# A SwiGLU feed-forward kernel: its first eight accumulation groups ordered by contraction step, with loads cut to match

## The chip, the core and the metric

The kernel runs on one core of a Trainium2 chip. The metric is device time in microseconds (us) of one execution; the number to be predicted is the median of the runs of the changed kernel. TensorE (PE) multiplies matrices into PSUM, ScalarE (ACT) evaluates SiLU, VectorE (DVE) multiplies and copies, and SyncE (SP) issues DMAs.

## The reference

```python
B, S, D, F = 1, 2048, 512, 1376          # x: S x D; w_gate, w_up: D x F; w_down: F x D; all bfloat16
def reference(x, w_gate, w_up, w_down):
    g = silu(x @ w_gate)
    u = x @ w_up
    return (g * u) @ w_down
```

## The kernel before

Everything fits on the chip, and each input is loaded once. The tokens are cut into four chunks of 512 (index `c`), the hidden size F into ten full tiles of 128 columns (index `ft`) and a rest of 96, the contraction over D into four steps of 128 (index `dk`; the changed kernel's text calls it k).

**Up-projection.** For each chunk `c` and tile `ft`, PE makes two accumulation groups of four matmuls each: the gate group G (line 179) and the up group U (line 191). One matmul takes a 128x128 block of `w_sb` as its weights and streams 512 columns of `xT_sb`, the transposed x, into one PSUM bank. ACT turns a G bank into SiLU in `sg_sb` (line 261); DVE multiplies that by the U bank and writes `hT_sb` (line 284). G groups use banks 0 to 2 in turn, U groups banks 3 and 4. The order is four matmuls of G, then four of U, tile by tile. The rest of 96 columns is packed with part of w_up in one more group X per chunk (line 204), and two groups Y at the end (lines 215 and 220).

**Down-projection.** For each of the 16 token tiles of 128, PE accumulates eleven matmuls over F into bank 6 or 7 in turn (line 245), DVE copies the bank to `o_sb` (line 308), and SP stores it (line 156). The last token tile is done in two halves of 256 columns; ACT copies the first half (line 275).

**The start.** PE first runs `N_WARM = 11` matmuls on constants (line 167), which need no data. ACT loads its SiLU table and evaluates it once on a dummy (line 254). SP alone issues all loads, in this order: the transposing load of the first chunk of x, whole, 512 x 512 (line 128); then w_gate and w_up alternately in slabs of 1, 1, 2, 3 and 4 tiles, each slab with all four contraction steps (lines 116 and 123); 32 columns of w_up (line 140); the other three chunks of x; w_down in two DMAs (lines 145 and 146). Each load has a semaphore of its own, and PE waits for x's chunk and for a slab before its first matmul with it. So PE's first real matmul needs the whole first chunk of x (512 KB) and the first slab of w_gate (128 KB); the engines work through their programs in the written order, and nothing reorders the groups.

Of the kernel before, what the change touches and what calls it, by code (L numbers as in the profile page):

```python
# [9 lines left out]
N_WARM = 11  # L10


def bass_standalone__swiglu_ffn__prompt_kernel(nc, x, w_gate, w_up, w_down, out):
# [4 lines left out]
    NFT = (F + P - 1) // P  # L18
    NFF = F // P
    F_LAST = F - NFF * P  # L20
# [5 lines left out]
    assert D == 512 and S % SC == 0 and KD == 4 and TPC == 4 and F_LAST == 96 and NSC % 2 == 0  # L26
# [4 lines left out]
    UPT = F  # L31
# [4 lines left out]

    slabs = [(0, 1), (1, 2), (2, 4), (4, 7), (7, NFT)]
    slab_of = {}
    for si, (a, b) in enumerate(slabs):
        for ft in range(a, b):  # L40
            slab_of[ft] = si

    with ExitStack() as es:
# [9 lines left out]
        NSG = 3  # L53
# [3 lines left out]
        NOS = 3  # L57
        o_sb = [sb(f"o_sb{i}", [P, D], BF16) for i in range(NOS)]

        banks = [ps(f"bank{i}", [P, 512], FP32) for i in range(8)]  # L60
        NG = 3
        psG = [banks[0], banks[1], banks[2]]
        NU = 2
        psU = [banks[3], banks[4]]
        psX = banks[5]
        NO = 2
        psO = [banks[6], banks[7]]
        psY = [banks[0], banks[1]]

        s_xT = [sem(f"s_xT{c}") for c in range(NSC)]  # L70
        s_wg = [sem(f"s_wg{i}") for i in range(len(slabs))]
        s_wu = [sem(f"s_wu{i}") for i in range(len(slabs))]
        s_wut = sem("s_wut")
        s_wd = sem("s_wd")
        s_G = sem("s_G")
        s_U = sem("s_U")
        s_Gf = sem("s_Gf")
        s_Uf = sem("s_Uf")
        s_X = sem("s_X")
        s_Xa = sem("s_Xa")  # L80
        s_Xd = sem("s_Xd")
        s_Y = sem("s_Y")
        s_Yd = sem("s_Yd")
        s_O = sem("s_O")
        s_Of = sem("s_Of")
        s_Ofa = sem("s_Ofa")
        s_out = [sem(f"s_out{i}") for i in range(NOS)]

# [4 lines left out]
        o_groups = []  # L93
        for t in range(NST):
            if t == NST - 1:
                o_groups.append((t, 0, HD))
                o_groups.append((t, HD, HD))
            else:
                o_groups.append((t, 0, D))
        NOG = len(o_groups)  # L100

        NGU = NSC * NFF
        gu_list = [(c, ft) for c in range(NSC) for ft in range(NFF)]

        def og_buf(gi):
            return o_groups[gi][0] % NOS

        def yblk(c):
            return (0, 64) if c % 2 == 0 else (64, 128)

        block = es.enter_context(nc.Block(no_gpsimd_drain=True))

        def wg_slab_dma(eng, si):
            a, b = slabs[si]
            f0, f1 = a * P, min(b * P, F)
            return eng.dma_start(
                w_sb[:, :, f0:f1], w_gate[:, f0:f1].rearrange("(k p) f -> p k f", p=P)
            ).then_inc(s_wg[si], 16)

        def wu_slab_dma(eng, si):  # L120
            a, b = slabs[si]
            f0, f1 = a * P, min(b * P, F - 32)
            return eng.dma_start(
                w_sb[:, :, UPH + f0:UPH + f1], w_up[:, f0:f1].rearrange("(k p) f -> p k f", p=P)
            ).then_inc(s_wu[si], 16)

        def xT_dma(eng, c):
            return eng.dma_start_transpose(
                xT_sb[:, :, c * SC:(c + 1) * SC], xf[c * SC:(c + 1) * SC, :]
            ).then_inc(s_xT[c], 16)  # L130

        WD_TOTAL = 32

        @block.sync
        def _(sp):
            xT_dma(sp, 0)
            for si in range(len(slabs)):
                wg_slab_dma(sp, si)
                wu_slab_dma(sp, si)
            sp.dma_start(  # L140
                w_sb[:, :, UPT:UPT + 32], w_up[:, F - 32:F].rearrange("(k p) f -> p k f", p=P)
            ).then_inc(s_wut, 16)
            for c in range(1, NSC):
                xT_dma(sp, c)
            sp.dma_start(wd_sb[:, 0:NFF, :], w_down[0:NFF * P, :].rearrange("(k p) d -> p k d", p=P)).then_inc(s_wd, 16)
            sp.dma_start(wd_sb[0:F_LAST, NFF, :], w_down[NFF * P:F, :]).then_inc(s_wd, 16)
            n_store = [0] * NOS
            for gi, (t, c0, ncol) in enumerate(o_groups):
                ob = og_buf(gi)
                if gi == NOG - 2:  # L150
                    sp.wait_ge(s_Ofa, 1)
                elif gi == NOG - 1:
                    sp.wait_ge(s_Of, gi)
                else:
                    sp.wait_ge(s_Of, gi + 1)
                sp.dma_start(of[t * P:(t + 1) * P, c0:c0 + ncol], o_sb[ob][:, c0:c0 + ncol]).then_inc(s_out[ob], 16)
                n_store[ob] += 1
            for i in range(NOS):
                sp.wait_ge(s_out[i], 16 * n_store[i])

        @block.tensor
        def _(pe):
            seen_g = set()
            seen_u = set()
            seen_x = set()
            for i in range(N_WARM):
                pe.matmul(banks[7][:, :], lhsT=ones_w, rhs=ones_m, start=True, stop=True)  # L167
            n = 0
            for c in range(NSC):
                pe.wait_ge(s_xT[c], 16)  # L170
                for ft in range(NFF):
                    si = slab_of[ft]
                    if si not in seen_g:
                        pe.wait_ge(s_wg[si], 16)
                        seen_g.add(si)
                    if n >= NG:
                        pe.wait_ge(s_Gf, n - NG + 1)
                    for dk in range(KD):
                        ins = pe.matmul(  # L179
                            psG[n % NG][:, :], lhsT=w_sb[:, dk, ft * P:(ft + 1) * P],  # L180
                            rhs=xT_sb[:, dk, c * SC:(c + 1) * SC],
                            start=(dk == 0), stop=(dk == KD - 1),
                        )
                    ins.then_inc(s_G, 1)
                    if si not in seen_u:
                        pe.wait_ge(s_wu[si], 16)
                        seen_u.add(si)
                    if n >= NU:
                        pe.wait_ge(s_Uf, n - NU + 1)
                    for dk in range(KD):  # L190
                        ins = pe.matmul(  # L191
                            psU[n % NU][:, :], lhsT=w_sb[:, dk, UPH + ft * P:UPH + (ft + 1) * P],
                            rhs=xT_sb[:, dk, c * SC:(c + 1) * SC],
                            start=(dk == 0), stop=(dk == KD - 1),
                        )
                    ins.then_inc(s_U, 1)
                    n += 1
                if c == 0:
                    pe.wait_ge(s_wg[slab_of[NFT - 1]], 16)
                    pe.wait_ge(s_wut, 16)  # L200
                else:
                    pe.wait_ge(s_Xd, c)
                for dk in range(KD):
                    ins = pe.matmul(  # L204
                        psX[:, :], lhsT=w_sb[:, dk, XC0:XC0 + P],
                        rhs=xT_sb[:, dk, c * SC:(c + 1) * SC],
                        start=(dk == 0), stop=(dk == KD - 1),
                    )
                ins.then_inc(s_X, 1)
            pe.wait_ge(s_wu[slab_of[NFT - 1]], 16)  # L210
            pe.wait_ge(s_Gf, NGU)
            for pi in range(NSC // 2):
                a, b = 2 * pi, 2 * pi + 1
                for dk in range(KD):
                    pe.matmul(  # L215
                        psY[pi][0:64, :], lhsT=w_sb[:, dk, YC0:YC0 + 64],
                        rhs=xT_sb[:, dk, a * SC:(a + 1) * SC],
                        start=(dk == 0), stop=(dk == KD - 1), tile_position=(0, 0), skip_group_check=True,
                    )
                    ins = pe.matmul(  # L220
                        psY[pi][64:128, :], lhsT=w_sb[:, dk, YC0:YC0 + 64],
                        rhs=xT_sb[:, dk, b * SC:(b + 1) * SC],
                        start=(dk == 0), stop=(dk == KD - 1), tile_position=(0, 64), skip_group_check=True,
                    )
                ins.then_inc(s_Y, 1)
            pe.wait_ge(s_wd, WD_TOTAL)
            seen_c = set()
            for gi, (t, c0, ncol) in enumerate(o_groups):
                bb = gi % NO
                c = t // TPC  # L230
                if c not in seen_c:
                    pe.wait_ge(s_Uf, NFF * (c + 1))
# [104 lines left out]
```

## Time and profile before

| | |
|---|---|
| three timed runs | 122.66, 122.89 and 123.19 us; median 122.89 us |
| the profiled execution: first to last instruction (span) | 121.1 us |
| its own time from outside | not given; the median run lies 1.74 us above the span |
| PE busy | 117.9 us, 97% of the span, 550 matmuls |
| DVE, ACT busy | 43.8 us (36%), 30.2 us (25%) |
| DMA | 8.42 MB on one queue, nearly all loads in the first fifth of the span |
| granted TensorE clock | 1.000 |

The profile is one execution on the chip. "PEld" rows are the weight loads that precede matmuls; "SPq" rows are DMA issues on SP's queue. A DMA's "us to landing" runs from its issue to the arrival of its last byte's signal. Matmuls are pipelined: a row's duration is longer than the pitch at which matmuls follow each other, and the pitch is what adds up to time.

### The profile page before, as it was taken

To read this page: it belongs to the slowest core of one execution; us is meant where nothing else is said; L and a number is where in the kernel's file an instruction comes from. 1 tells how busy PE (TensorE), PEld (TensorE's weight loads), DVE (VectorE), ACT (ScalarE), POOL (GpSimd) and SP (SyncE) were. 2 spreads that over 40 slices of the span, in tenths; PEclk is the share of its full clock that TensorE was granted. 3 is DMA by queue.
4 is the path that set the end of the run, shared out by engine and by line. 5 is a ranking of instruction groups with operands and counts; after the bars stand their busy time and mean duration, and the time that the engine had idled before them with its cause. 6 is when DMAs were issued, how large, how long until landed. Compare 5 with 4: busy or idle time off the path is not lost.

```text
span 121.1 us, 1391 instructions
## 1 busy us (share of the span) xinstructions
PE 117.9 (97%) x550; PEld 53.3 (44%) x550; DVE 43.8 (36%) x64; ACT 30.2 (25%) x51; POOL 0.2 (0%) x4
## 2 busy tenths in 40 slices
PE   7999999999999999999999999999999999999991
PEld 2244444444444444444444444444444444444470
DVE  0024334444334444334444334467242233224221
ACT  4032333262333272333262333230000000000010
POOL 0000000000000000000000000000000000000000
PEclk9999999999999999999999999999999999999999
DMA  3999999900000000000000000000211211121121
GB/s 67 255 283 372 262 241 225 369 20 0 0 0 0 0 0 5 0 0 3 3 0 0 0 0 0 5 0 0 87 43 43 87 43 49 49 81 43 43 74 56
DMA packets 17990, 8.51 MB, mean 70 GB/s; under 512 B 11360, under 2 KB 17984, under 8 KB 17984
## 3 DMA queue, kind: packets, MB, share of 16 engines
q1 hardware_dynamic: 17984, 8.42, 25.6%
q8 instruction: 4, 0.07, 0.2%
q14 instruction: 2, 0.02, 0.0%
HBM read 4.23 MB, written 2.10 MB: 52 GB/s over the span
## 4 chain that ended last, share of the span: by engine, by line
PE 97%; DVE 0%; issue 0%
PE bank L245 32%; PE bank L179 29%; PE bank L191 29%; PE bank L167 4%; PE bank L204 3%; PE bank L215 2%; DVE o_sb L308 0%; PE bank L220 0%
## 5 line engine op out<-in xcount | busy, mean ns | idle before, releaser
L284 DVE TENSOR_TENSOR hT_sb<-sg_sb,bank 128x512 bf16<-128x512 f32 x40 | 27.5, 688 | 44.9 <-PE bank L191 44.8
L179 PE MATMUL bank<-xT_sb,w_sb 128*128 128x512 bf16 x160 | 41.5, 382 | 0.0
L191 PE MATMUL bank<-xT_sb,w_sb 128*128 128x512 bf16 x160 | 41.1, 379 | 0.0
L245 PE MATMUL bank<-wd_sb,hT_sb 128*128 128x512 bf16 (+3 forms) x187 | 38.3, 367 | 0.0
L261 ACT ACTIVATE sg_sb<-bank 128x512 f32<-128x512 f32 x40 | 23.8, 596 | 44.7 <-PE bank L179 44.7
L245 PEld LDWEIGHTS bank<-wd_sb,hT_sb 128*128 128x128 bf16 (+1 forms) x187 | 18.1, 97 | 20.3 <-issue 0.4
L179 PEld LDWEIGHTS bank<-xT_sb,w_sb 128*128 128x128 bf16 x160 | 15.6, 98 | 19.8 <-DMA xT_sb<-in_x_dram 0.8
L191 PEld LDWEIGHTS bank<-xT_sb,w_sb 128*128 128x128 bf16 x160 | 15.6, 98 | 18.9
L308 DVE CAST o_sb<-bank 128x512 bf16<-128x512 f32 (+1 forms) x16 | 10.8, 675 | 24.9 <-PE bank L245 24.9
L275 ACT ACTIVATE o_sb<-bank 128x256 bf16<-128x256 f32 x1 | 0.4, 383 | 37.6 <-PE bank L245 37.6
L167 PE MATMUL bank<-const-bfloat16-1.0 128*128 128x512 bf16 x11 | 4.9, 628 | 0.8 <-PEq L322 0.8
L289 DVE TENSOR_TENSOR hT_sb<-sgx_sb,bank 32x512 bf16<-32x512 f32 x4 | 2.8, 692 | 5.3 <-ACT sgy_sb L266 5.3
L204 PE MATMUL bank<-xT_sb,w_sb 128*128 128x512 bf16 x16 | 4.1, 379 | 0.0
L265 ACT ACTIVATE sgx_sb<-bank 32x512 f32<-32x512 f32 x4 | 2.4, 588 | 4.5 <-PE bank L204 4.5
L167 PEld LDWEIGHTS bank<-const-bfloat16-1.0 128*128 128x128 bf16 x11 | 1.5, 140 | 3.3 <-issue 3.3
L296 DVE TENSOR_TENSOR hT_sb<-sgy_sb,bank 64x512 bf16<-64x512 f32 x4 | 2.7, 684 | 0.1
L204 PEld LDWEIGHTS bank<-xT_sb,w_sb 128*128 128x128 bf16 x16 | 1.6, 98 | 1.9
L266 ACT ACTIVATE sgy_sb<-bank 64x512 f32<-64x512 f32 x4 | 2.4, 589 | 0.0
L215 PE MATMUL bank<-xT_sb,w_sb 128*64 128x512 bf16 x8 | 1.9, 382 | 0.0
L220 PE MATMUL bank<-xT_sb,w_sb 128*64 128x512 bf16 x8 | 1.9, 382 | 0.0
L254 ACT ACT_TABLE_LOAD x1 | 1.3, 1283 | 0.7 <-PEq L322 0.7
L215 PEld LDWEIGHTS bank<-xT_sb,w_sb 128*64 128x64 bf16 x8 | 0.8, 110 | 1.0 <-issue 0.4
(6 smaller groups left out, 1.4 us busy)
## 6 DMA issues: line engine op xcount, KB each, us to landing
out_dram<-o_sb SPq DMA_DIRECT2D x15, 128.0 KB, 1.7
wd_sb<-in_w_down_dram SPq DMA_DIRECT2D x1, 1280.0 KB, 6.3
w_sb<-in_w_gate_dram SPq DMA_DIRECT2D x1, 480.0 KB, 6.2
w_sb<-in_w_up_dram SPq DMA_DIRECT2D x1, 448.0 KB, 6.8
w_sb<-in_w_gate_dram SPq DMA_DIRECT2D x1, 384.0 KB, 4.8
w_sb<-in_w_up_dram SPq DMA_DIRECT2D x1, 384.0 KB, 5.4
w_sb<-in_w_gate_dram SPq DMA_DIRECT2D x2, 128.0 KB, 3.1
w_sb<-in_w_up_dram SPq DMA_DIRECT2D x2, 128.0 KB, 3.0
```

What stands on the lines that cost most here:

```text
L167: pe.matmul(banks[7][:, :], lhsT=ones_w, rhs=ones_m, start=True, stop=True)
L179: ins = pe.matmul(psG[n % NG][:, :], lhsT=w_sb[:, dk, ft * P:(ft + 1) * P], rhs=xT_sb[:, dk, c * SC:(c + 1) * SC], start=(dk == 0), stop=( ...
L191: ins = pe.matmul(psU[n % NU][:, :], lhsT=w_sb[:, dk, UPH + ft * P:UPH + (ft + 1) * P], rhs=xT_sb[:, dk, c * SC:(c + 1) * SC], start=(dk = ...
L204: ins = pe.matmul(psX[:, :], lhsT=w_sb[:, dk, XC0:XC0 + P], rhs=xT_sb[:, dk, c * SC:(c + 1) * SC], start=(dk == 0), stop=(dk == KD - 1),)
L215: pe.matmul(psY[pi][0:64, :], lhsT=w_sb[:, dk, YC0:YC0 + 64], rhs=xT_sb[:, dk, a * SC:(a + 1) * SC], start=(dk == 0), stop=(dk == KD - 1), ...
L245: ins = pe.matmul(psO[bb][:, 0:ncol], lhsT=hT_sb[0:K, fk, t * P:(t + 1) * P], rhs=wd_sb[0:K, fk, c0:c0 + ncol], start=(fk == 0), stop=(fk ...
L261: act.activation(sg_sb[n % NSG][:, :], psG[n % NG][:, :], ACT.Silu).then_inc(s_Gf, 1)
L265: act.activation(sgx_sb[c][96:128, :], psX[64:96, :], ACT.Silu)
L284: dve.tensor_tensor(hT_sb[:, ft, c * SC:(c + 1) * SC], sg_sb[n % NSG][:, :], psU[n % NU][:, :], ALU.mult,).then_inc(s_Uf, 1)
L289: dve.tensor_tensor(hT_sb[64:96, NFF, c * SC:(c + 1) * SC], sgx_sb[c][96:128, :], psX[96:128, :], ALU.mult,).then_inc(s_Xd, 1)
L296: dve.tensor_tensor(hT_sb[0:64, NFF, c * SC:(c + 1) * SC], sgy_sb[c][y0:y1, :], psY[pi][y0:y1, :], ALU.mult,).then_inc(s_Yd, 1)
L308: dve.tensor_copy(o_sb[ob][:, c0:c0 + ncol], psO[bb][:, 0:ncol]).then_inc(s_Of, 1)
```

## The change

The first eight groups (G and U of tiles 0 to 3 of chunk 0; `N_HEAD = 4`) run contraction step by contraction step: step 0 of all eight groups, each into a bank of its own, then step 1, and so on. In steps 0 to 2 the four G matmuls come ahead of the four U matmuls; in the last step the order is G, U, G, U as before. Their loads are cut the same way, by step: x's first chunk comes in three transposing DMAs (step 0, step 1, steps 2 and 3; 128, 128 and 256 KB), issued by SP; the weights of the four tiles come in six DMAs (gate and up for step 0, step 1, steps 2 and 3; 128, 128, 128, 128, 256, 256 KB, rows of 1 KB), issued by ACT ahead of its table load. SP goes on with the slabs of tiles 4 to 5, 6 to 7 and 8 to 10, and then as before.

After the head, every group of the program (G, U, X, Y and the down-projection's O) takes the next of all eight banks in turn, and PE waits for whoever read the group eight places earlier. Three counters (`s_P`, `s_A`, `s_D`) replace the separate semaphores between engines. `sg_sb` has four buffers in place of three, and `N_WARM` is 6 in place of 11. The number of matmuls, activations and vector operations on data is the same, and so is the order of the groups after the head.

The diff, cut to its core:

```diff
-N_WARM = 11
+N_WARM = 6
+N_HEAD = 4
...
-        NSG = 3
+    NSG = 4
...
-        psG = [banks[0], banks[1], banks[2]]
-        psU = [banks[3], banks[4]]
-        psX = banks[5]
-        psO = [banks[6], banks[7]]
-        psY = [banks[0], banks[1]]
...
+        def load_x(eng, name, c, k0, k1):
+            eng.dma_start_transpose(
+                xT_sb[:, k0:k1, c * SC:(c + 1) * SC], xf[c * SC:(c + 1) * SC, k0 * P:k1 * P]
+            ).then_inc(load_sem(name), 16)
+
+        def load_w(eng, name, src, base, k0, k1, f0, f1):
+            eng.dma_start(
+                w_sb[:, k0:k1, base + f0:base + f1],
+                src[k0 * P:k1 * P, f0:f1].rearrange("(k p) f -> p k f", p=P),
+            ).then_inc(load_sem(name), 16)
+
+        head_k = [(0, 1), (1, 2), (2, 4)]
+        slabs = [(4, 6), (6, 8), (8, NFT)]
+
+        def loads_on_scalar(act):
+            for k0, k1 in head_k:
+                load_w(act, f"wg_h{k0}", w_gate, 0, k0, k1, 0, HC)
+                load_w(act, f"wu_h{k0}", w_up, UPH, k0, k1, 0, HC)
...
+        def loads_on_sync(sp):
+            for k0, k1 in head_k:
+                load_x(sp, f"x0_{k0}", 0, k0, k1)
+            for a, b in slabs:
+                load_w(sp, f"wg_{a}", w_gate, 0, 0, KD, a * P, min(b * P, F))
+                load_w(sp, f"wu_{a}", w_up, UPH, 0, KD, a * P, min(b * P, F - 32))
...
+        def add_group(kind, **what):
+            g = dict(kind=kind, at=len(groups), bank=banks[len(groups) % NB], readers=[], **what)
...
+        @block.scalar
+        def _(act):
+            loads_on_scalar(act)
+            act.activation(adummy[:, 0:4], zero_c, ACT.Silu)
...
+            def free(g):
+                if g["at"] >= NB:
+                    for eng, n in groups[g["at"] - NB]["readers"]:
+                        after(eng, n)
...
             for i in range(N_WARM):
-                pe.matmul(banks[7][:, :], lhsT=ones_w, rhs=ones_m, start=True, stop=True)
...
+                pe.matmul(banks[NB - 1][:, :], lhsT=ones_w, rhs=ones_m, start=True, stop=True)
+
+            head = groups[:2 * N_HEAD]
+            for dk in range(KD):
+                order = head if dk == KD - 1 else head[0::2] + head[1::2]
+                for g in order:
+                    gu_matmul(g, dk)
+
+            for g in groups[2 * N_HEAD:]:
+                free(g)
```

## The prediction

> **What bounds the kernel now.** I read the chain of waits first, as a total, then in order of time.
>
> ```profile
> PE 97%; DVE 0%; issue 0%
> 0.77 4.85 PE bank L167 x11
> 5.62 1.33 PE bank L179 x4
> 6.96 0.86 PE bank L191 x4
> 7.82 0.86 PE bank L179 x4
> 80.46 38.21 PE bank L245 x187
> 118.69 0.42 DVE o_sb L308
> ```
>
> The columns are start, length, what. From 6.96 us to 118.67 us PE is never late: four matmuls take 0.863 us, a pitch of 0.216 us, and 187 matmuls of the down-projection take 38.21 us. No other engine and no load stands in the chain before the last copy. A change that keeps the number of matmuls can win only ahead of 6.96 us, or lose anywhere. So I read the start in the timeline (start, length, engine, line).
>
> ```profile
> 0.74 1.40 SPq L128 DMA_TRANSPOSE xT_sb<-in_x_dram  x1
> 2.20 0.66 SPq L116 DMA_DIRECT2D w_sb<-in_w_gate_dram  x1
> 2.44 0.15 PEld L167 LDWEIGHTS bank<-const-bfloat16-1.0 128*128 128x128 bf16 x1 [0.28 <-issue]
> 2.86 0.15 PEld L167 LDWEIGHTS bank<-const-bfloat16-1.0 128*128 128x128 bf16 x1 [0.28 <-issue]
> 5.54 1.42 PE L179 MATMUL bank<-xT_sb,w_sb 128*128 128x512 bf16 x4
> 6.35 0.61 PE L179 MATMUL bank<-xT_sb,w_sb 128*128 128x512 bf16 x2
> ```
>
> The last row is a narrow window; the third real matmul starts there. Warm-up matmuls follow each other at 0.427 us; from 6.35 us on the pitch is 0.216 us. So PE runs at half pace for the first 5.6 us after its first matmul (0.77), and the first real one starts at 5.54 us, after the eleventh warm-up (0.77 + 11 x 0.427 = 5.47). The slab of w_gate, issued at 2.20, landed 3.2 us later, at 5.4; x, issued at 0.74, landed after 4.2 us, at 4.94. Warm-ups and data end together: taking warm-ups away alone brings nothing.
>
> Third, the stretches of the DMA engines (PE, PEld, DVE, ACT, POOL busy, then clock, DMA share, GB/s).
>
> ```profile
> 1.50:2.10 0.60, 0.60 (x3) 0.24 (x2) 0.00 (x0) 0.59 (x2) 0.00 (x0) 1.00 0.00 0
> 2.10:2.50 0.40, 0.40 (x3) 0.12 (x2) 0.00 (x0) 0.13 (x1) 0.00 (x0) 1.00 0.76 181
> 2.50:3.00 0.50, 0.50 (x3) 0.22 (x2) 0.00 (x0) 0.00 (x0) 0.00 (x0) 1.00 1.18 246
> 3.00:4.00 1.00, 1.00 (x4) 0.30 (x3) 0.00 (x0) 0.00 (x0) 0.00 (x0) 1.00 1.27 289
> 19.75:20.50 0.75, 0.75 (x5) 0.39 (x4) 0.56 (x1) 0.00 (x0) 0.00 (x0) 1.00 1.07 142
> 21.50:23.50 2.00, 2.00 (x11) 0.94 (x10) 0.79 (x2) 0.60 (x1) 0.00 (x0) 1.00 1.07 379
> ```
>
> The first byte moves at 2.1 us, 1.4 us after the issue of x. Transposed x moves at 246 to 289 GB/s; w_down, in rows of 1 KB, at 379, after a slow 142 just behind the last transpose. Adding up from 2.1 us, x's 524 kB are through by 4.2 us, so a transpose lands about 0.75 us after its last byte.
>
> **When the head can start.** Its first matmul needs 131 kB of x and 131 kB of w_gate, issued side by side at about 0.74 us by SP and ACT. The first byte: between 0.84 us after the issue (a store issued at 86.08 moves nothing until 86.9) and the 1.4 us of the whole transpose; so 1.6 to 2.1 us. I take 1.9, since a quarter of a transpose is nearer to the small DMA. The moving: 0.5 us if x has the engines to itself (131 kB at 270 GB/s), 1.0 if the two pieces share them evenly, 2.4 if all four weight pieces of steps 0 and 1 (524 kB) get ahead of x's first; I take 1.0, because the pieces that follow are issued 0.55 us apart (2.20, 2.92, 3.45, 4.00 on SP's queue). With the 0.75 us tail: 1.9 + 1.0 + 0.75 = 3.65 us, with ends of 2.85 and 5.25. The six warm-ups end at 0.77 + 6 x 0.427 = 3.33, which is the floor.
>
> **What that is worth.** With the full pace from 6.35 us as now, a real matmul done before it costs no time at full pace. Now 1.9 matmuls fall there ((6.35 - 5.54) / 0.427); with a start at 3.65, 6.3. The difference, 4.4 x 0.216 = 0.96 us, comes off the end. The floor of 3.33 gives 1.1 us; a start at 5.25 gives 0.15.
>
> **Whether the loads keep up behind it.** With that start, step 0 ends at 6.7 us, step 1 at 8.4, step 2 at 10.2 and step 3 at 11.9 (eight matmuls, 1.73 us each). All of x's chunk and the step 2 gate weights are wanted at 8.4, the up weights at 9.3. The head's 1,573 kB from 2.1 us at 280 GB/s, with the tail, are there at 8.5 if SP's slabs stay behind x on their queue. At 379 GB/s for the 1 KB rows and 270 for x it is 7.6; if ACT's last pieces share with SP's next two slabs (524 kB more at 270) it is 10.6 and PE stalls 1.3 us. I take no stall, since ACT's six issues are over by 4 us and its rows are longer; the 1.3 us stay in the range.
>
> ACT's six issues, 0.55 us each, end near 4.0; table load (1.28 us) and dummy (0.20) then end near 5.6 in place of 2.2. The first SiLU is wanted near 10.4, when the first G of step 3 is done, so this costs nothing; it would if the head ended 5 us earlier. SP loses six issues and gains two.
>
> **The join after the head.** The eight banks fill within 1.73 us, and ACT and DVE then have four tiles at once. Say the head's last matmul ends at T. The first G ends near T - 1.5, its SiLU (0.60 us, starting 0.2 us later as now) at T - 0.7; its bank is wanted at T. The first product (0.69 us) ends at T + 0.03, its bank is wanted at T + 0.86. Each further tile is wanted 1.73 us later and needs 0.60 and 0.69. No stall; if ACT were a full 0.7 us late, PE would begin to wait.
>
> **The rest.** Eight banks in turn give later groups at least the slack they have, and now PE waits for none of them. Deadlines of slabs and of x's second chunk (wanted near 23 us, issued near 9.65 now, landed 6.7 us later) keep several us. Down-projection and last store are the same: nothing. The merged counters are waits on work several groups old: nothing, bounded by the gaps in the chain, 0.02 us at most.
>
> **Sum.** Span 121.1 - 0.96 = 120.2 us. The median run lies 1.74 us above the span of the profiled execution, which gives 121.9 us.
>
> [...] In the trace, half pace lasted 5.6 us through matmuls without a gap over 0.15 us; no row shows what a gap does. [...]
>
> **Rivals.**
>
> *Loads mixed on two queues run slower (slower than before).* For: behind the last transpose, copies moved at 142 GB/s, under two fifths of 379; the change puts transposes and copies on the engines together. Against: at 4 to 5 us, copies followed a transpose at 230. Price: at 142 GB/s the head's 1,573 kB land at 2.1 + 11.1 + 0.75 = 13.9; the up half of step 2 and all of step 3 (2.6 us) follow, so the head ends at 16.5. Now the same 32 matmuls end at 12.85 (30.1 x 0.216 after 6.35). That is 3.7 us lost, 126.5 us. It decides from the point where the last piece lands after 10.3, an average below 212 GB/s.
>
> *The gap delays full pace.* With data at 3.65, PE stands 0.3 us. From the rows: if the 5.6 us start over with the first real matmul, full pace comes at 9.25. Each us of delay costs 0.49 us, so 1.43 - 0.96 = 0.5 us lost, 123.4 us; with a start at 4.5, 1.3 us lost, 124.2. Against: five warm-ups more or less are no long idle.
>
> *The data come late, nothing worse.* A start between 4.4 and 5.25, or a stall up to 1.3 us at step 2, leaves -0.6 to +0.4 us: 122.3 to 123.3. It is also the case in which ordering by step doesn't do what it says, because x's first piece lands with the rest.
>
> **Chances.** The forecast (start before 4.4, no stall) 0.55. Late data 0.15, within 0.5%. The gap 0.13, of it 0.05 within 0.5% and 0.08 slower. Mixed loads 0.17, slower. Half a per cent (0.61 us) is about what a measurement of this kernel can tell from no change. So faster 0.55, same 0.20, slower 0.25. The forecast's own range, with the spread of the runs (-0.23, +0.30), is 121.5 to 122.5. The range to 123.6 takes in late data and the milder half of the gap, and leaves out most of the mixed loads and the dearer gap, 0.2.
>
> **What would show it.** Right: first real matmul near 3.65 us, pitch doubling near 6.35, no idle PE after that, last matmul near 117.7. Wrong: pitch doubling near 9 or later (the gap); PE idle on a load at 8 to 14 us, with under 212 GB/s in those stretches (mixed loads); first real matmul after 4.4 (late data); any PE wait on ACT or DVE behind the head.

## The result, and the profile after

The changed kernel takes 124.16 us (median; 123.75 to 124.43) against 122.88 us for the kernel before: slower by a ratio of 1.0095, with a 95% interval of 1.0073 to 1.0117. The predicted 121.9 us had the wrong sign, and the range of 121.5 to 123.6 us does not hold the time. The profiled execution took 124.23 us, with a span of 122.5 us. (Times and ratios in this document leave out single runs that lie over 1.5% above the fastest of their kernel.)

The chain of waits after (start, length, what):

```profile
PE 93%; DMA 4%; issue 1%; DVE 0%
0.73 4.78 DMA xT_sb<-in_x_dram
5.51 0.05 issue
5.55 11.13 PE bank L278 x43
...
120.00 0.42 DVE o_sb L245
```

A load has entered the chain: x's first piece, issued at 0.73, lands at 5.51 us. So the first real matmul starts at 5.55 us, where it started before (5.54), although it now needs only a quarter of x's first chunk. The last copy starts at 120.00 in place of 118.69 us. The 1.31 us between the two is lost behind the first matmul. The timeline after shows where:

```profile
0.73 3.87 SPq L74 DMA_TRANSPOSE xT_sb<-in_x_dram  x3
0.77 2.72 PE L286 MATMUL bank<-const-bfloat16-1.0 128*128 128x512 bf16 x6 [0.77 <-PEq L351]
5.55 19.12 PE L278 MATMUL bank<-xT_sb,w_sb 128*128 128x512 bf16 x79 [2.07 <-DMA xT_sb<-in_x_dram]
8.09 0.15 PEld L278 LDWEIGHTS bank<-xT_sb,w_sb 128*128 128x128 bf16 x1 [0.28 <-issue]
8.52 0.15 PEld L278 LDWEIGHTS bank<-xT_sb,w_sb 128*128 128x128 bf16 x1 [0.28 <-issue]
8.94 15.23 PEld L278 LDWEIGHTS bank<-xT_sb,w_sb 128*128 128x128 bf16 x71 [0.28 <-issue]
12.84 2.06 ACT L233 ACTIVATE sg_sb<-bank 128x512 f32<-128x512 f32 x4 [7.26 <-PE bank L278]
13.54 3.22 DVE L241 TENSOR_TENSOR hT_sb<-sg_sb,bank 128x512 bf16<-128x512 f32 x5 [13.54 <-PE bank L278]
```

PE stands for 2.07 us between the sixth warm-up and the first real matmul. Then weight loads still follow each other at 0.43 us up to 8.94; only from there do they come in one dense row. In the matmul records the ninth real matmul, at 8.94 us, is the first at about full pace (the tenth follows at 9.18; before, it was the third, at 6.35, with the next at 6.58). Up to the tenth, nine matmuls take 3.63 us, where full pace would take 9 x 0.216 = 1.94, so 1.69 us is lost. Before, three matmuls took 1.04 us (5.54 to 6.58), 0.39 us lost. The difference, 1.30 us, is the whole slowdown of this execution (its span is 1.30 us longer). Behind the head, ACT takes four SiLUs back to back and DVE five products, and PE waits for neither.

The landings of the first loads after, each from the DMA view of a narrow stretch (the last number is us from issue to landing). The x rows are the pieces issued at 0.73, 2.01 and 3.31 us; the second row is the first gate piece.

```profile
xT_sb<-in_x_dram SPq DMA_TRANSPOSE x1, 4.8
w_sb<-in_w_gate_dram ACTq DMA_DIRECT2D x1, 128.0 KB, 2.3
xT_sb<-in_x_dram SPq DMA_TRANSPOSE x1, 5.0
xT_sb<-in_x_dram SPq DMA_TRANSPOSE x1, 6.7
```

The two transposes of 128 KB took 4.8 and 5.0 us, longer than the 4.2 us of the whole 512 KB before. The stretches after (last three numbers: clock, DMA share, GB/s):

```profile
2.50:3.00 0.50, 0.50 (x3) 0.07 (x1) 0.00 (x0) 0.00 (x0) 0.00 (x0) 1.00 1.21 290
3.50:4.00 0.50, 0.00 (x0) 0.00 (x0) 0.00 (x0) 0.00 (x0) 0.00 (x0) 1.00 0.64 140
4.00:4.50 0.50, 0.00 (x0) 0.00 (x0) 0.00 (x0) 0.42 (x1) 0.00 (x0) 1.00 1.37 182
4.50:5.00 0.50, 0.00 (x0) 0.00 (x0) 0.00 (x0) 0.50 (x1) 0.00 (x0) 1.00 1.05 137
5.00:5.50 0.50, 0.00 (x0) 0.00 (x0) 0.00 (x0) 0.49 (x2) 0.00 (x0) 1.00 0.91 144
```

From 3.5 to 5.5 us the DMA engines are occupied (shares of 0.64 to 1.37) and move about half of the 290 GB/s of the first row. In the packet records 501 of the first piece's 512 packets have begun by 3.0 us; its landing comes 2.5 us later, where before it took about 0.75.

### The profile page after: what moved, and what is told of

Its sections match the earlier page's. It is cut to its first block, busy times and chain, and to the rows that moved or that the text cites. A ratio compares the mean times of both kernels' runs of the same rounds, so it can differ in the third digit from the quotient of the medians.

```text
span 122.5 us, 1383 instructions
## 1 busy us (share of the span) xinstructions
PE 116.5 (95%) x535; PEld 52.9 (43%) x545; DVE 43.5 (36%) x64; ACT 29.9 (24%) x51; POOL 0.2 (0%) x4
## 3 DMA queue, kind: packets, MB, share of 16 engines
q10 hardware_dynamic: 1120, 1.05, 4.1%
## 4 chain that ended last, share of the span: by engine, by line
PE 93%; DMA 4%; issue 1%; DVE 0%
PE bank L278 58%; PE bank L333 31%; DMA xT_sb<-in_x_dram 4%; PE bank L305 3%; PE bank L316 2%; DVE o_sb L245 0%
## 5 line engine op out<-in xcount | busy, mean ns | idle before, releaser
L278 PE MATMUL bank<-xT_sb,w_sb 128*128 128x512 bf16 x314 | 71.1, 385 | 2.4 <-DMA xT_sb<-in_x_dram 2.1
L305 PE MATMUL bank<-xT_sb,w_sb 128*128 128x512 bf16 x16 | 4.1, 379 | 0.0
L286 PE MATMUL bank<-const-bfloat16-1.0 128*128 128x512 bf16 x6 | 2.7, 623 | 0.8 <-PEq L351 0.8
L316 PE MATMUL bank<-xT_sb,w_sb 128*64 128x512 bf16 x16 | 1.9, 382 | 0.0
L286 PEld LDWEIGHTS bank<-const-bfloat16-1.0 128*128 128x128 bf16 x6 | 0.7, 133 | 1.8 <-issue 1.8
```

The lines of the kernel that those rows point to most:

```text
L278: ins = pe.matmul(g["bank"][:, :], lhsT=w_sb[:, dk, col:col + P], rhs=xT_sb[:, dk, c * SC:(c + 1) * SC], start=(dk == 0), stop=(dk == KD - 1),
L286: pe.matmul(banks[NB - 1][:, :], lhsT=ones_w, rhs=ones_m, start=True, stop=True)
L305: ins = pe.matmul(g["bank"][:, :], lhsT=w_sb[:, dk, XC0:XC0 + P], rhs=xT_sb[:, dk, c * SC:(c + 1) * SC], start=(dk == 0), stop=(dk == KD - 1),
L316: ins = pe.matmul(g["bank"][y0:y1, :], lhsT=w_sb[:, dk, YC0:YC0 + 64], rhs=xT_sb[:, dk, c * SC:(c + 1) * SC], start=(dk == 0), stop=(dk == ...
```

## The experiments

The theory has two parts. (M): copies from ACT's queue, in flight beside a transpose, hold up its completion. (G): the late landing leaves PE idle, and that idleness, not the late start, makes the half pace last longer. The rivals: (T) a quarter of a transpose is slow by itself; the order by step, eight banks or counters cost something; the idle time does not matter.

### Covering the idle time

```diff
-N_WARM = 6
+N_WARM = 11
```

> The changed kernel with N_WARM = 11 in place of 6, nothing else. Theory (the gap between the last warm-up and the first real matmul keeps PE at half pace for longer, and that alone is the loss): the warm-ups end at 5.47 us, the first real matmul stays near 5.55, the pitch halves near 6.35 us as in the kernel before, and the time falls by 1.3 us to 122.9 us, equal to the kernel before. Rival (ordering by step, the eight banks or the merged counters cost something themselves): the pitch halves early but the time stays above 123.5 us.

Measured: 123.35 us, beside 122.68 us for the kernel before on the same chip; ratio 1.0057 (1.0035 to 1.0079). So half of the loss comes back and 0.7 us stays. The PE timeline:

```profile
5.41 3.85 PE L278 MATMUL bank<-xT_sb,w_sb 128*128 128x512 bf16 x16
9.72 1.47 PE L278 MATMUL bank<-xT_sb,w_sb 128*128 128x512 bf16 x6 [0.45 <-DMA xT_sb<-in_x_dram]
```

The start is at 5.41 us and full pace is there from the second real matmul on (5.84 us), as G expected. But now sixteen matmuls, steps 0 and 1, are through before x's third piece has landed, and PE stands: 0.83 us from one matmul to the next in place of 0.22. That 0.61 us is nearly all that stays. In the changed kernel the same late piece cost nothing, since PE was late itself. The theory was right about the idle time and missed the second cost that it covered.

### The kernel before, with six warm-ups

```diff
-N_WARM = 11
+N_WARM = 6
```

(in the kernel before)

> The kernel before with N_WARM = 6 in place of 11, nothing else: the loads are untouched, so the first real matmul stays near 5.5 us and PE stands from 3.33 to 5.5 us. Theory (a stand of 2 us makes the half pace last some 3 us longer): eight or so real matmuls run at 0.427 us instead of two, and the time rises by about 1.3 us to 124.0 us. Rival (the stand does not matter, or full pace comes at a fixed time): the pitch halves near 6.35 us again and the time stays at 122.7 us.

Measured: 124.3 us (122.78 to 124.58), ratio 1.011 (1.0081 to 1.0139). Its timeline:

```profile
5.81 1.87 PE L179 MATMUL bank<-xT_sb,w_sb 128*128 128x512 bf16 x4 [2.33 <-DMA w_sb<-in_w_gate_dram]
7.47 1.73 PE L191 MATMUL bank<-xT_sb,w_sb 128*128 128x512 bf16 x4
8.75 0.60 PEld L179 LDWEIGHTS bank<-xT_sb,w_sb 128*128 128x128 bf16 x3 [0.28 <-issue]
```

The first eight real matmuls go at half pace, to about 9.0 us, with nothing changed but five warm-ups fewer. Idle for 2.3 us, this kernel loses as much as the changed one, without its loads and its order: the rival of a full pace that comes at a fixed time whatever PE does is out. One of its twelve executions took 122.78 us and lost nothing, so the loss is frequent and not certain. Both this run and the one above change the number of warm-ups together with the idle time; no run keeps six warm-ups and takes the idle time away, so G is shown for the two together.

### A transpose with nothing beside it

```diff
         def loads_on_scalar(act):
+            act.wait_ge(loads["x0_0"], 16)
```

(the changed kernel with N_WARM = 11; in the next two kernels the same wait stands behind the first, or the first two, of ACT's loads)

> N_WARM = 11, and ACT issues its six weight loads only after x's first piece has landed, so that this transpose runs with no copy beside it. Theory M (copies from the other queue running beside a transpose hold up its completion): the first piece, issued at 0.73 us, lands near 3.5 us instead of 5.5 us (last packet near 2.75, then a tail of about 0.75 us). Rival T (a transposing DMA of a quarter takes 4.8 us to land by itself): it lands at 5.5 us again. The time of the whole run is not what this run is for; it is expected to be longer than 122.9 us, since the weights are issued near 3.6 us or later.

> The changed kernel with N_WARM = 11, ACT issuing the step 0 gate weights at once and its other five loads only after x's first piece has landed: 128 KB of copies beside the first transpose. One look at when that piece lands (5.5 us in the changed kernel, 4.9 with 11 warm-ups, 3.4 with no copy beside it). If the delay comes from what is in flight behind and between its packets: 3.4 to 3.6 us, since this copy is through when the transpose's last packets are. If any copy from the other queue costs its full length: 4.0 us or more. The whole run is expected at 123.5 us or more, since the up weights come late.

> As e9_one_beside, but ACT issues gate and up weights of step 0 (256 KB) at once and holds the other four. If the delay grows with the copies that are still moving after the transpose's last packet: the piece lands at 3.8 to 4.5 us, between the two. If it is a matter of one copy or none: as in e9_one_beside.

The landing row of the first piece of x, in the kernel with nothing beside it, and ACT's first issue, which waits for that landing:

```profile
xT_sb<-in_x_dram SPq DMA_TRANSPOSE x1, 2.7
3.44 0.40 ACTq L79 DMA_DIRECT2D w_sb<-in_w_gate_dram  x1
```

And with 256 KB beside it:

```profile
xT_sb<-in_x_dram SPq DMA_TRANSPOSE x1, 3.7
```

From issue to landing, by what ACT has issued meanwhile (each a profiled execution):

| first transpose | nothing | 128 KB | 256 KB | all six loads |
|---|---|---|---|---|
| quarter, 128 KB | 2.7 us | 2.7 us | 3.7 us | 4.2 us (11 warm-ups), 4.8 us (the changed kernel) |
| half, 256 KB (versions further down) | not run | 3.5 us | 4.3 us | |
| whole, 512 KB (runs further down) | 4.2 us (before) | 4.2 us | 5.0 us (rows of 1 KB), 5.2 us (rows of 256 B) | |

The first copy, through by 2.6 us, costs nothing. The second makes the landing slip by 0.8 to 1.0 us, the other four by another 0.5 to 1.1. T is out: by itself a quarter has landed by 3.44 us.

The trace also shows where the slip arises, and there M holds for the quarter alone. Behind a transpose's data the trace has 32 packets of four bytes, and then the signals of its landing. For the quarter, the last of these packets begins at 2.94 us with nothing beside it, at 2.98 with 128 KB and at 3.38 to 3.48 with more; from there to the landing it takes 0.48, 0.48, then 1.05 us (256 KB) and 1.6 to 2.0 us (all six). So most of its slip lies behind its data: the completion is held up. For the whole transpose the packets themselves come later (4.37 us before, 4.40 with 128 KB, 5.22 and 5.29 with 256 KB), and 0.55 to 0.63 us remain in every case: there it is moved more slowly, and its completion takes as long as ever.

The three kernels of this section took 124.82, 124.45 and 124.70 us, one execution each; the weights then come late and PE stands in the head.

### Two slabs on ACT in the kernel before

```diff
-            for si in range(len(slabs)):
+            for si in range(1, len(slabs)):
                 wg_slab_dma(sp, si)
...
+            wg_slab_dma(act, 0)
+            wu_slab_dma(act, 0)
             act.activation(adummy[:, 0:4], zero_c, ACT.Silu)
```

> The kernel before (11 warm-ups, no ordering by step), with the first slab of w_gate and of w_up (128 KB each, rows of 256 B) issued by ACT ahead of its table load instead of by SP behind x. Theory M: the copies run beside the one transpose of x and delay its landing from 4.94 us to 5.5 us or more; the start moves by 0 to +1 us and the time is 122.9 to 123.5 us. Rival T (the transposes are slow only because they are cut into pieces): x lands at 4.9 to 5.1 us, the slab of w_gate no longer binds, the start stays behind the warm-ups at 5.5 us, and the time is 122.7 to 122.9 us.

Measured: 122.98 us, ratio 1.0014 (1.0001 to 1.0028), and x landed at 5.92 us, 5.2 us after its issue. T's landing at 4.9 to 5.1 us did not come. The weights delay a whole transpose too, though by slowing its data: a second queue for the weights gains nothing if the weights hold up x.

### One queue for all

```diff
+                load_w(sp, f"wg_h{k0}", w_gate, 0, k0, k1, 0, HC)
+                load_w(sp, f"wu_h{k0}", w_up, UPH, k0, k1, 0, HC)
```

(behind each `load_x` of the head; none on ACT; N_WARM = 11)

> N_WARM = 11, and SP issues all the head's loads on its one queue: each piece of x, then the gate and up weights of the same step. Theory M (mixing of transposes and copies in flight is what costs, whichever queue they come from): the first piece of x lands before 4.5 us, the step 0 gate weights near 5 us, and the head starts near 5.2 us; the later pieces of x follow copies and are delayed, and if x's third piece lands after 9 us PE stalls. Time 122.5 to 123.5 us. Rival (it is the second queue, not the mixing): all pieces land at the rate of the kernel before (1,573 kB at 230 to 290 GB/s, the last near 9 us), no stall, and the time is 122.4 to 122.8 us.

Measured: 124.0 us, ratio 1.0098 (1.0065 to 1.013), beyond both expectations. The first piece landed 2.7 us after its issue, with copies close behind it on its own queue: such copies did not hold it up. (They started when the piece's data were through: the engines moved 165 GB/s from 2.45 to 2.80 us, 4 to 3.15 and 135 to 3.50. No run puts copies of SP's own queue between a transpose's packets, so that it is the second queue and not the mixing stays open.) The rest failed elsewhere, as PE's waits show (us in total, times, longest):

```profile
PE bank L284 <- DMA w_sb<-in_w_gate_dram: 2.3, 2, 2.0
```

Each transposing DMA occupied SP for 1.14 to 1.26 us, and in this order the third is issued only at 5.38 us and the step 2 gate weights at 6.69. PE waits 2.0 us for these.

### The order by step alone

```diff
+        x_k = [(0, 4)]
+        on_act = []
...
-            for k0, k1 in head_k:
+            for k0, k1 in x_k:
                 load_x(sp, f"x0_{k0}", 0, k0, k1)
+            load_head(sp, False)
```

(the changed kernel with N_WARM = 11; `x_k` has the pieces of x, `on_act` the weight loads that ACT issues; `load_head` has SP issue the others behind x)

> The changed kernel's order by step, its eight banks and counters, but x's first chunk in one transposing DMA and the head's six weight loads behind it on SP's queue, and N_WARM = 11. Theory (only the loads and the missing warm-ups cost): x lands near 4.94 us, the step 0 gate weights near 5.4, the start is at 5.5 us, no load is waited for after that, and the time is 122.6 to 122.8 us like the kernel before. Rival (ordering by step, eight banks or counters cost): 123.2 us or more with the same start.

Measured: 122.68 us, ratio 0.999 (0.9973 to 1.0007).

```profile
5.52 1.46 PE L286 MATMUL bank<-xT_sb,w_sb 128*128 128x512 bf16 x6 [0.16 <-DMA w_sb<-in_w_gate_dram]
```

The start is where it was, and there is no further wait for a load. The order, the banks, the counters and the join together cost nothing that this measurement can tell, and bring nothing: what the change lost lies in how it loads and in its number of warm-ups.

### Versions built on this

```diff
-        on_act = []
+        on_act = ['wg_h0']
```

(otherwise as the order alone, N_WARM = 10: the gate weights of step 0 on ACT, the other five loads on SP behind x)

> As e6_order_alone, but ACT issues the step 0 gate weights (128 KB, rows of 1 KB) ahead of its table load, and N_WARM = 10. Those packets should be through by 2.5 us, so that they meet x's transpose only at its beginning. Theory M (a copy delays a transpose only while both are in flight): x lands by 5.1 us, the start is at 5.1 to 5.2 us, and the time is 122.5 us, 0.2 us under the kernel before. Rival (any copy beside the transpose delays it by a microsecond, as the two slabs on ACT did): x lands at 5.9 us, the start moves to 6 us, 122.9 us or more.

Measured: 122.22 us, ratio 0.995 (0.9935 to 0.9966): faster than the kernel before, and the lowest median of all. x lands 4.2 us after its issue, undisturbed, and the gate piece is there long before:

```profile
0.72 0.38 ACTq L79 DMA_DIRECT2D w_sb<-in_w_gate_dram  x1
0.73 1.41 SPq L74 DMA_TRANSPOSE xT_sb<-in_x_dram  x1
5.01 2.30 PE L286 MATMUL bank<-xT_sb,w_sb 128*128 128x512 bf16 x6
```

The first real matmul starts at 5.01 us, half a microsecond earlier, with no idle PE in between. (This profiled execution was the slowest of the eleven, 122.85 us: in it full pace came only at 6.70 us. The other ten took 122.03 to 122.53.)

> As e7_gate_first (122.22 us), but ACT issues the step 0 up weights ahead of its table load too: 256 KB in rows of 1 KB beside the one transpose of x. Nothing waits for the up weights in e7, so no gain can come from this. If the second copy, still moving between the transpose's packets, delays x: x lands 0.2 to 1 us later than 4.95 us and the time is 122.3 to 122.8 us. If not: 122.2 us.

The second piece on ACT takes the gain away again: 122.89 us, ratio 1.0007 (0.9994 to 1.002), x landing 0.8 us later:

```profile
xT_sb<-in_x_dram SPq DMA_TRANSPOSE x1, 5.0
```

In its profiled execution the tenth warm-up follows the ninth by 0.25 us, near full pace. PE then stood for over a microsecond, to 5.82 us, and the first real matmuls still went at full pace: there, idle time after full pace had come did no harm.

The same with x in two pieces:

```diff
-        x_k = [(0, 4)]
+        x_k = [(0, 2), (2, 4)]
```

(with the gate piece alone on ACT, N_WARM = 7; then with both step 0 pieces on ACT, N_WARM = 8)

> As e7_gate_first, but x's first chunk in two transposing DMAs (steps 0 and 1, steps 2 and 3), N_WARM = 7, and all other weights behind both on SP's queue. Theory M: the first piece lands near 4.0 us and the four step 0 gate matmuls run from there; the up weights of step 0 land near 5.8 us, so PE stands at most 0.3 us; some three more real matmuls than in the kernel before run ahead of 6.35 us, and the time is 122.0 to 122.4 us. Rival (issue and completion of two transposes cost more than they give): the second piece and the weights behind it come after 6.5 us, PE stands for a microsecond or more, and the time is 123 us or more.

> As e8_two_pieces, but ACT issues the step 0 up weights too, and N_WARM = 8, so that the wait for them (PE stood from 4.93 to 6.29 us for it) goes. The copies beside the first transpose double. If the first piece still lands by 4.5 us: start near 4.5, eight step 0 matmuls without a stand, 122.0 to 122.3 us. If the second copy delays it past 5 us: start near 5.1, 122.5 us or more.

With the gate piece alone on ACT: 122.99 us, ratio 1.0041 (1.0008 to 1.0073), spread from 122.57 to 124.36. The rival held: the head starts at 4.27 us, but the up weights come behind two transposes.

```profile
4.27 1.04 PE L286 MATMUL bank<-xT_sb,w_sb 128*128 128x512 bf16 x4 [0.36 <-DMA xT_sb<-in_x_dram]
6.29 0.61 PE L286 MATMUL bank<-xT_sb,w_sb 128*128 128x512 bf16 x2 [0.98 <-DMA w_sb<-in_w_up_dram]
```

With both on ACT: 122.24 us, ratio 0.9961 (0.9942 to 0.9981): faster than before, and in the median not to be told from the one-piece version. But three of the twelve executions took 124.03 to 124.20 us. The profiled one is among them: x's first piece landed at 4.99 us, 0.8 us later than with the gate piece alone, PE stood for 0.70 us behind eight warm-ups, and ten real matmuls went at half pace, to 9.2 us. So this version still loses, in one execution of four, what the changed kernel lost.

## Why the prediction was wrong, step by step

**When the head can start: this step failed.** The sum was 1.9 + 1.0 + 0.75 = 3.65 us, with an upper end of 5.25; measured 5.51. First byte and moving were about right (through by about 3.0 us). The term that broke was the tail: 0.75 us was read from a transpose whose followers stood on its own queue, and it became 2.5 us with another queue's copies in flight. With nothing beside it the piece had landed by 3.44 us, between the sum with 0.5 us of moving (3.15) and the 3.65. The row that I used was sound, but for another situation, and my upper end let the copies only go ahead of x's bytes, not hold up its end.

**SP's issues: a term left out.** I counted SP's issues and put no duration on the transposes among them. (The count was off too: ten slab loads became six, so SP lost four issues, not six. x's second chunk was issued at 11.41 us in place of 9.65, and PE did not wait for it.) The pieces took 1.23, 1.25 and 1.29 us to issue, hardly less than the whole (1.40). So the third piece is issued at 3.31 us and lands at 10.0, where "there at 8.5" was expected. In the changed kernel this is hidden behind a late PE; with the idle time covered it costs 0.61 us.

**The gap: the right mechanism, given 0.13.** The price rule for it holds: full pace at 8.94 in place of 6.35 us, at 0.49 us lost for each microsecond, gives 1.27 us, and 1.30 was measured. The failure is that I priced the gap at 0.3 us idle, from my own start time, and "late data" as if PE's pace did not depend on it. The two are one case: each microsecond by which the data is late is a microsecond of idle PE, because the change removes five warm-ups. "Taking warm-ups away alone brings nothing" was the sentence to follow up; taken away alone, they cost 1.1% (ratio 1.011). That the rival's dearer figure, 124.2 us, stands beside the measured 124.16 is luck: it took a start at 4.5 us and 5.6 us of half pace from there, where 5.55 and 3.4 were measured.

The half pace behind the first real matmul lasted 3.4 us in the changed kernel (5.55 to 8.94) and 3.2 us in the kernel before with six warm-ups (5.81 to 9.04). The sum put 0.96 us down as won by an earlier start with full pace where it was; measured, the start won nothing (5.55 in place of 5.54) and full pace came 2.6 us later (8.94 in place of 6.35).

**Mixed loads: the mechanism was there, in another place.** The DMA engines moved 137 to 182 GB/s from 3.5 to 5.5 us. But the head's last pieces had landed by 10.0 us, ahead of the 10.3 from which I let this case decide, and PE did not stall at step 2. What the mixing decided, it decided at the first piece.

**What held.** ACT's table load and dummy ended at 5.58 us (5.6 expected) and nobody waited. The join, the eight banks, the counters and the rest cost nothing, alone too (ratio 0.999).

## What to carry to other kernels

Cutting a load into pieces lets work start earlier only if the first piece lands earlier: ask what else is in flight when its last packet is through (here a quarter took 2.7 us to land with nothing beside it and 4.8 with six copies), and how long each further piece occupies the issuing queue (here 1.23 to 1.29 us). Here one copy that was over when the transpose's packets had only begun gained 0.5%, and a second one lost all of it. Let warm-up matmuls reach to the first data: here six of them with 2 us of idle PE behind cost 1.1% in the kernel before. Size them by the measured landing and, if in doubt, one too many: one more can delay the start by no more than its 0.43 us.

## What the runs showed of the hardware that was not expected

Copies on the same queue behind a transpose left its landing alone (2.7 us for a quarter, 4.2 for a whole one); 256 KB or more of copies from the other queue put it off by 0.8 to 2.1 us, and 128 KB that were through early did not. The signals in the trace, sixteen for each landing, tell how: in the changed kernel ten of the first piece's come at 4.04 to 4.18 us, directly behind those of ACT's second copy (3.79 to 4.03), four more by 4.88, and the last two at 5.29 and 5.51. So at the end PE waited for two signals of sixteen. For the quarter, 1.05 to 2.0 us lay between its last packet and its landing with 256 KB or more beside it, in place of 0.48; for the whole transpose, 0.55 to 0.63 us in every case. Why the completion is held up, no run here shows.

The time of full pace varied. With the same eleven warm-ups, the eight from 2.00 us on took 3.62 us in the changed kernel with 11 warm-ups and 2.67 us in the one with a single queue (PE timeline to 6.7 us of each):

```profile
2.00 3.62 PE L286 MATMUL bank<-const-bfloat16-1.0 128*128 128x512 bf16 x8
```

```profile
2.00 2.67 PE L292 MATMUL bank<-const-bfloat16-1.0 128*128 128x512 bf16 x8
```

In the second, full pace came at about 3.6 us, in the kernel before at 6.35. Nor did it come after a fixed number of matmuls: seven went at half pace ahead of it in the second, thirteen in the kernel before, and eighteen in the version with two pieces and both weight pieces on ACT. What sets the moment, no run here shows. The times spread too: those of the kernel before with six warm-ups cover 1.8 us, those of the version with the gate piece first 0.8 us.
